# Banded attention and a dropless mixture of experts on one core: attention in steps of two units, the gate once per batch, and a fixed second expert whose weights are fetched into attention memory

## The chip, the core and the metric

The kernel runs on one core of one Trainium2 chip. A core has five engines that run their own instruction streams and meet at semaphores: TensorE (PE, matrix products; its weight loads are shown apart as PEld), VectorE (DVE), ScalarE (ACT), GpSimd (POOL) and SyncE (SP, which here only issues DMAs). Sixteen DMA engines move data between the device memory and the on-chip memory.

The metric is the device time of one execution in microseconds (us), lower is better; a kernel's time is the median of three executions. The profile comes from one further execution with the hardware profiler on.

## What is computed

The reference, cut to what matters. All numbers are float32.

```python
B, H, S, D = 4, 8, 768, 64            # batch, heads, tokens, head size
scores = q @ k.T / sqrt(D)            # per batch and head
keep = (key < n_global) | (0 <= query - key < n_local)     # 8 global keys, 96 local keys
scores += -slope[h] * dist            # dist = query-key, or n_local for a global key that is not local
a = softmax(where(keep, scores, -1e9)); attn = a @ v
x = attn.transpose(0, 2, 1, 3).reshape(3072, 512)          # one row per token

logits = x @ w_gate                   # 512 x 8
e = argmax(logits); gate = softmax(logits)[e]              # one expert of 8 for each token
y = relu(x @ w1[e]) @ w2[e]           # 512 -> 1024 -> 512, for the tokens of each expert
out = gate * y
```

Each expert gets as many tokens as chose it. With the given inputs the counts of experts 0 to 7 are 455, 416, 361, 397, 367, 410, 395 and 271. The kernel has fixed capacities `CAPS = (464, 416, 416, 400, 400, 368, 368, 272)` and a general, slower path behind a test, which these inputs do not take in either version.

## The kernel before

**Attention.** A unit is (batch b, pair of heads j, two blocks of 128 queries c); there are 4 x 4 x 3 = 48 units. `scores(n)` makes transposed scores, keys on partitions, with 64-row matmuls for the two heads; ACT takes the exponential and DVE multiplies by the bias-and-mask factors. `attend(n)` multiplies by the values (full 128-row matmuls), and DVE divides by the sums. `turn(n)` transposes the unit's output with the identity for the gate. Units are worked one at a time, each stage some units behind the one before:

```python
for n in range(nu + 1):                          # nu = 48
    if c == 1: load(pr + 3)                      # q and k of a pair of heads, pr = 4*b + j
    scores(n)
    turn(n - 4)
    logits(n - 5)                                # acts only where j == 3: three units of a batch
    attend(n - 2)
    logits_sum(n - 5)                            # likewise
    if c == 0: turn_qk(pr + 1)                   # two DVE transposes of the loaded q and k
    if c == 1: keys_at(...)                      # ACT copies
    if c == 2: turn_v(pr + 1)                    # ACT copies
    if c == 1: load_v(pr + 2)
    # one batch later, at units 6 and 8 of the batch:
    spread(b2); spread_sum(b2)
```

**Gate and places.** For each group of 256 tokens, four products of 32 columns each, side by side in the array, give partial logits, ACT copies them, and two more products with a 0/1 matrix add the four parts. `gate(b)` then runs once for a batch on DVE. `spread(b)` finds each token's place in its expert's list:

```python
def logits(n):
    for kc in range(KC):                         # KC = 4
        nc.tensor.matmul(pq[32*kc:32*kc+32, :], lhsT=wg_sb[:, kc, :], rhs=xl[:, kc, :])  # 256 columns
    nc.scalar.copy(out=lq, in_=pq)
def logits_sum(n):
    for t in range(2):
        nc.tensor.matmul(pl[:, t, :], lhsT=lq[:, P*t:P*t+P], rhs=gsum)
    nc.vector.tensor_copy(out=Ls[b][:, 2*c:2*c+2, :], in_=pl)
    if c == NB // 2 - 1: gate(...)
def spread(b):                                   # NB = 6 blocks of 128 tokens
    nc.tensor.matmul(pr, lhsT=tri, rhs=Mb, start=True, stop=False)
    for c in range(NB - 1):
        nc.tensor.matmul(pr[:, c+1:NB, :], lhsT=ones, rhs=Mb[:, c:c+1, :] ...)   # five products
    if b > 0: nc.tensor.matmul(pr, lhsT=ones, rhs=Macc ...)                      # counts of earlier batches
    # ... DVE: positions, then the tables mv and oh for spread_sum
```

**End of attention.** The tokens of expert 0 that are known after three batches are gathered early, and their work is cut into 16 pieces that fill TensorE while the routing of the last batch is worked out on DVE. POOL issues a gather of 32 rows per indirect DMA.

```python
            spread_sum(B - 1); half_0(1); order()        # order: experts 1..7 ranked by their counts
            work(1); fetch_0(1); settle(); work(1)
            rows_of(...); take(1)                        # 13 gathers for the expert that comes second
            identify(); sort_acc(1, gslot_s); fit(); work(5)
            turn_x(...); work(4)
```

**Experts.** Two sets of weight tiles take turns. `w1_second` and `w2_second` lie in a pool that is opened after attention's pools are closed, so in memory that attention used.

```python
def fetch(p, i):                       # i = 0: w1, four DMAs of 512 KB; i = 1: w2, one of 2 MB
    ids[p] = nc.values_load(ids_s[...])          # which expert, read from memory by SP
    if i == 0:
        loads = expert_w1(ws[p % 2][0], bass.ds(ids[p], 1))
        if p == 1: behind(loads[0], taken[len(taken) // 2], ...)   # after the 7th of the 13 gathers
    else: nc.sync.dma_start(ws[p % 2][1], ...)
def sort(p):                           # DVE transposes of the gathered rows of expert p
    turn_x(xes[p], xqs.pop(p), pieces_of(CAPS[ORDER[p]]))

fetch(1, 0); fetch(1, 1); ground(); sort(1)
hidden(0); plan(2); turn = result(0)             # the rest of expert 0: 208 slots
for p in range(1, E):
    hidden(p, turn)                    # 8 x 4 matmuls, ACT relu; pace() lets gathers out one by one
    fetch(p + 1, 0)
    sort(p + 1)
    plan(p + 2)
    turn = result(p)                   # 4 x 8 matmuls, DVE copies yT, then transposes and scatter
    fetch(p + 1, 1)
```

Of the kernel before, what the change touches and what calls it, by code (L numbers as in the profile page):

```python
# [29 lines left out]
def kernel(  # L30
# [27 lines left out]

    x_tok = nc.dram_tensor("x_tok", (N * NJ, P), F32)
# [22 lines left out]
    q_first = consts.tile([P, NB, 2, D], F32)  # L82
# [48 lines left out]

    tokid = consts.tile([P, NC], F32)
    iota(tokid, [[P, NC]], -N, 1)
# [5 lines left out]
    def later_constants():  # L139
# [13 lines left out]
        nc.vector.tensor_copy(out=j_of, in_=j_i)  # L153
        nc.vector.memset(wg_sb, 0.0)
        nc.sync.dma_start(wg_sb[:, :, 0:E], moe_w_gate.rearrange("(kc p) e -> p kc e", p=P))

    gsum = sel[:, 0:E]

    M_ec = consts.tile([P, E, NC], F32)
    M_ce = consts.tile([P, NC, E], F32)  # L160
    rk_all = consts.tile([P, NB, E + 1], F32)
    nc.vector.memset(rk_all[:, :, E:E + 1], 0.5)
    Macc = consts.tile([P, E], F32)
# [8 lines left out]
    NR = E - 1  # L172
# [5 lines left out]
    idx_0 = [consts.tile([P, 1, 2], I32, name=f"idx_0{i}") for i in range(2)]  # L178
    gslot_0 = [consts.tile([P, 1, 2], F32, name=f"gslot_0{i}") for i in range(2)]
    rows_0 = [consts.tile([P, 2 * TB], I32, name=f"rows_0{i}") for i in range(2)]  # L180
# [93 lines left out]
    def plan(p):  # L274
        if p < E:
            r = ORDER[p] - 1
            xqs[p] = xq_s[p % 2]
            cols = rows_s[:, NQ * TB * r:NQ * TB * r + NQ * TB]
            for i in range(pieces_of(CAPS[r + 1])):
                pending.append((xqs[p], cols, i))  # L280
# [10 lines left out]
    taken = []  # L291

    def take(p):
        plan(p)
        while pending:
            taken.append(gather_one(*pending.pop(0)))

    scatters = []

# [24 lines left out]
    def result_0(po, q, f0, nf, later=None):  # L324

        for fc in range(f0, f0 + nf):
            nc.tensor.matmul(po, lhsT=hT_0[q][:, fc, :], rhs=w2_0[:, 0, fc, :],  # L327
                             start=(fc == 0), stop=(fc == FC - 1))
        if f0 + nf == FC:
            scaled(f"y_0_{q}", P, po, gslot_0[0][:, 0, q:q + 1], idx_0[0][:, 0, q:q + 1], later)  # L330
# [18 lines left out]
    def banded_attention():  # L349
        with ExitStack() as actx:  # L350
            mp = actx.enter_context(tc.tile_pool(name="maskb", bufs=1))
            xlp = actx.enter_context(tc.tile_pool(name="xlb", bufs=3))
            xrp = actx.enter_context(tc.tile_pool(name="xrb", bufs=5))
            ldp = actx.enter_context(tc.tile_pool(name="ldb", bufs=2))
# [3 lines left out]
            xp = actx.enter_context(tc.tile_pool(name="xpb", bufs=3))  # L358
# [17 lines left out]
            def load(pr):  # L376
                b, j = divmod(pr, NJ)
                ts = []
                for nm, src in (("q", q), ("k", k)):
                    t = ldp.tile([P, S // 32, 32], F32, tag=nm, name=f"{nm}b_{pr}")  # L380
# [65 lines left out]
            far = mp.tile([P, 2, P], F32, name="farb")  # L446
# [18 lines left out]
            Ls = {}  # L465
            xls = {}
# [6 lines left out]
            def scores(n):  # L473
# [12 lines left out]
                e = ep.tile([P, 2, 512], F32, tag="e", name=f"e_{n}")  # L486
# [40 lines left out]
            def turn(n):  # L527
                b, j, c = units[n]
                xr = xrs[b, c]
                px = ps_m.tile([P, 2, P], F32, tag="m", name=f"px_{n}")  # L530
                for t in range(2):
                    nc.tensor.transpose(px[:, t, :], xr[:, t, P * j:P * j + P], ident)  # L532
                if j == 0:
                    xls[b, c] = xlp.tile([P, KC, 2 * P], F32, tag="xl", name=f"xl_{b}_{c}")
                nc.scalar.copy(out=xls[b, c][:, j, :], in_=px.rearrange("p t c -> p (t c)"))
                if j == NJ - 1:
                    store(S * b + 2 * P * c, 2, xrs.pop((b, c)))

            def logits(n):

                b, j, c = units[n]
                if j < NJ - 1:
                    return
                xl = xls.pop((b, c))
                pq = ps_m.tile([P, 2 * P], F32, tag="m", name=f"pq_{n}")
                for kc in range(KC):
                    nc.tensor.matmul(pq[32 * kc:32 * kc + 32, :], lhsT=wg_sb[:, kc, :], rhs=xl[:, kc, :],  # L547
                                     start=True, stop=True)
                lq = xp.tile([P, 2 * P], F32, tag="lq", name=f"lq_{n}", bufs=2)
                nc.scalar.copy(out=lq, in_=pq)  # L550
                st["l", n] = lq

            def logits_sum(n):
                b, j, c = units[n]
                if j < NJ - 1:
                    return
                lq = st.pop(("l", n))
                pl = ps_m.tile([P, 2, E], F32, tag="m", name=f"pl_{n}")
                for t in range(2):
                    nc.tensor.matmul(pl[:, t, :], lhsT=lq[:, P * t:P * t + P], rhs=gsum, start=True, stop=True)  # L560
                if c == 0:
                    Ls[b] = gp.tile([P, NB, E], F32, tag="L", name=f"L_{b}")
                nc.vector.tensor_copy(out=Ls[b][:, 2 * c:2 * c + 2, :], in_=pl)
                if c == NB // 2 - 1:
                    gate(b, Ls.pop(b), gp, M_ce[:, NB * b:NB * b + NB, :])

            def spread(b):

                Mb = M_ce[:, NB * b:NB * b + NB, :]
# [3 lines left out]
                for c in range(NB - 1):  # L573
                    nc.tensor.matmul(pr[:, c + 1:NB, :], lhsT=ones,
                                     rhs=Mb[:, c:c + 1, :].to_broadcast([P, NB - 1 - c, E]),
                                     start=False, stop=(b == 0 and c == NB - 2))
                if b > 0:
                    nc.tensor.matmul(pr, lhsT=ones,
                                     rhs=Macc.rearrange("p (o e) -> p o e", o=1).to_broadcast([P, NB, E]),
                                     start=False, stop=True)  # L580
                Mt = gp.tile([P, 2, NB, E], F32, tag="Mt", name=f"Mt_{b}")
                for i, f in enumerate((tokid, gates)):
# [17 lines left out]
                                        op=ALU.is_equal)  # L600
                mv = gp.tile([P, NB, 2, E, NQ], F32, tag="mv", name=f"mv_{b}", bufs=1)
# [9 lines left out]
                Mv = Mb.rearrange("p c e -> p e c")  # L611
                if b == 0:
                    nc.vector.tensor_reduce(out=Macc, in_=Mv, axis=AX.X, op=ALU.add)
                else:
                    per = gp.tile([P, E], F32, tag="per", name=f"per_{b}")
                    nc.vector.tensor_reduce(out=per, in_=Mv, axis=AX.X, op=ALU.add)
                    nc.vector.tensor_tensor(out=Macc, in0=Macc, in1=per, op=ALU.add)
# [14 lines left out]
            def half_0(i):  # L632

                f = gp.tile([P, 1, 2], F32, tag="first", name=f"first_{i}")
                nc.vector.tensor_copy(out=f, in_=acc[:, 0, 0:1, 2 * i:2 * i + 2])
                st["w", i] = wrap(gp, f"_0{i}", 2, f[:, 0, :], idx_0[i][:, 0, :])
                nc.vector.tensor_copy(out=gslot_0[i], in_=acc[:, 1, 0:1, 2 * i:2 * i + 2])

            def fetch_0(i):
                rows_of(ps_m, f"_0{i}", 2, st.pop(("w", i)), rows_0[i])  # L640
# [4 lines left out]
            def count_0():  # L645
                c2 = ps_m.tile([P, E], F32, tag="m", name="c2")
                nc.tensor.matmul(c2, lhsT=ones, rhs=Macc, start=True, stop=True)
                nc.vector.tensor_scalar(out=early, in0=c2[:, 0:1], scalar1=2.0 * P, scalar2=None, op0=ALU.is_ge)  # L648

            fill = []  # L650
            later = []
# [21 lines left out]
            def order():  # L673

                cn = ps_m.tile([P, E], F32, tag="m", name="cn")
                nc.tensor.matmul(cn, lhsT=ones, rhs=Macc, start=True, stop=True)
# [5 lines left out]
                k7 = key[:, 1:E]  # L682
# [11 lines left out]
            def identify():  # L694
# [4 lines left out]
                                        in1=iota_p[0:1, 1:E].rearrange("p (o e) -> p o e", o=1).to_broadcast([1, NR, NR]),  # L699
# [4 lines left out]
            def sort_acc(i, to):  # L704
# [5 lines left out]
                    in1=acc[:, i, 1:E, :].rearrange("p e q -> p q e").rearrange("p (o q) e -> p o q e", o=1).to_broadcast([P, NR, NQ, NR]),  # L710
# [8 lines left out]
            def fit():  # L719
# [3 lines left out]
                nc.vector.tensor_copy(out=cs[:, 0:1], in_=cnt[:, 0:1])  # L723
                sized = gp.tile([P, NR, NR], F32, tag="cmp", name="sized")
                nc.vector.tensor_tensor(out=sized, in0=R,
                                        in1=cnt[:, 1:E].rearrange("p (o e) -> p o e", o=1).to_broadcast([P, NR, NR]),
                                        op=ALU.mult)
                nc.vector.tensor_reduce(out=cs[:, 1:E], in_=sized, axis=AX.X, op=ALU.add)
# [12 lines left out]
            weights_0 = [lambda f0=f0: nc.sync.dma_start(w2_0[:, :, f0:f0 + 1, :], w2v[:, 0:1, f0:f0 + 1, :]) for f0 in range(FC)]  # L741
            weights_0 += [lambda e=e, kc=kc: nc.sync.dma_start(w1_0[32 * e:32 * e + 32, :, kc:kc + 1, :], w1v[e, :, 0:1, kc:kc + 1, :])
                          for e in range(NJ) for kc in range(KC)]
            for n in range(nu + 1):
                if n < nu:
                    b, j, c = units[n]
                    pr = b * NJ + j
                    if c == 1 and pr + 3 < B * NJ:
                        load(pr + 3)
                    scores(n)  # L750
                    if n == 2:
                        later_constants()
                    if n % 3 > 0 and 8 <= n < 44:
# [3 lines left out]
                if 0 <= n - 4 < nu:  # L757
                    turn(n - 4)
# [417 lines left out]
```

## Time and profile before

| What | Value |
|---|---|
| Time, median of three executions | 543.34 us (543.27 to 544.06) |
| Execution with the profiler on | 556.98 us, of which 555.3 us from the first to the last instruction |
| Mean granted TensorE clock in it | 0.986 |
| PE busy, PEld busy | 527.4 us, 391.7 us |
| DVE, ACT, POOL busy | 201.7 us, 132.6 us, 138.3 us |
| Data moved | 71.97 MB, mean 130 GB/s |

The profile page gives the busy time of each engine, a strip of 40 time slices, the DMA queues, the chain of work that ended last, and the costliest groups of instructions. A group names the source line, the engine, the operation and the tiles; "idle before" is the time in which the engine had nothing to do just before those instructions, with what ended most of it. The trace behind the page answers narrower questions: who waited for whom, what each engine did in a stretch of time, and the chain of waits in order of time. The busy time of a matmul is taken from its start to a modelled end, so overlapping matmuls can fill a stretch in which the array is not at its peak; the distance from one start to the next says more.

The stages of this run: attention takes from the start to about 174 us, the end of attention with the pieces of expert 0 until about 214 us, and the rest of the experts until 548 us.

### The profile page before, as it was taken

The page shows a single profiled execution, that of the slowest core. Times are in us where ns is not written, and L with a number is a line of the kernel's source. Part 1 is how long each engine was busy: PE and PEld are TensorE (multiplying, and loading weights), DVE is VectorE, ACT ScalarE, POOL GpSimd, SP SyncE. Part 2 cuts the span into 40 slices and gives each one's busy share as a digit, 9 for nine tenths or more (in the row PEclk, how much of TensorE's full clock was granted, in tenths as well). Part 3 has the DMA queues.
Part 4 walks back from the last instruction along what each step waited for, and adds up shares of the span by engine and source line. Part 5 has one row for each costly group of instructions (what it writes and reads, how often), then busy time and mean ns, then how long its engine had stood idle before and what let it go on. Part 6 is the DMA issues. An engine that isn't in the chain of part 4 may idle for free.

```text
span 555.3 us, 8124 instructions
## 1 busy us (share of the span) xinstructions
PE 527.4 (95%) x3130; PEld 391.7 (71%) x3130; DVE 201.7 (36%) x509; ACT 132.6 (24%) x263; POOL 138.3 (25%) x161
## 2 busy tenths in 40 slices
PE   4999999999999998599999999999999999999994
PEld 3988898899898965595555555555555876666694
DVE  4758687687684443112013101211301303111012
ACT  4666456555552200101101100100110100101100
POOL 5000000000007067234224423513511716402002
PEclk9999999999999999699999999999999999999998
DMA  9999999999903014995446174372543776101001
GB/s 145 146 156 178 234 176 175 231 161 159 256 6 124 31 30 93 297 187 201 98 90 223 34 159 141 114 156 70 183 107 64 234 147 216 48 0 53 3 1 60
DMA packets 145185, 71.97 MB, mean 130 GB/s; under 512 B 126656, under 2 KB 126660, under 8 KB 145136
## 3 DMA queue, kind: packets, MB, share of 16 engines
q1 hardware_dynamic: 137344, 58.16, 50.0%
q0 software_dynamic: 5264, 12.59, 7.5%
q10 hardware_dynamic: 2528, 0.59, 0.7%
q8 instruction: 27, 0.44, 0.4%
q14 instruction: 22, 0.18, 0.1%
HBM read 59.00 MB, written 12.65 MB: 129 GB/s over the span
## 4 chain that ended last, share of the span: by engine, by line
PE 85%; DMA 5%; SPq 2%; issue 2%; DVE 2%; another core or an unknown queue 2%; POOL 1%; ACT 0%; POOLq 0%; DVEq 0%; ACTq 0%
PE po L1082 26%; PE ph L1039 26%; PE o L516 12%; PE s L484 7%; PE ph L320 3%; PE px L532 3%; PE po L327 2%; PE pt L1072 2%; SPq L384 2%; DMA xq_s<-x_tok,rows_s 2%; DMA kb<-in_k_dram 1%; PE pq L547 1%; PE pi L624 1%; PE pl L560 1%
## 5 line engine op out<-in xcount | busy, mean ns | idle before, releaser
L259 POOL DMA_INDIRECT xq_s<-x_tok,rows_s x85 | 85.4, 1005 | 151.4 <-DVE yT L1084 103.6
L1041 ACT ACTIVATE hT<-ph 128x416 f32<-128x416 f32 (+4 forms) x64 | 29.6, 467 | 294.3 <-PE ph L1039 270.1
L1039 PE MATMUL ph<-xe,w_first 128*128 128x208 f32 (+3 forms) x256 | 78.7, 465 | 8.9 <-ACT hT L1041 8.9
L1082 PE MATMUL po<-hT,w_second 128*128 128x416 f32 (+4 forms) x320 | 80.7, 412 | 2.1 <-DVE yT L1084 2.1
L1039 PE MATMUL ph<-xe,w_second 128*128 128x416 f32 (+3 forms) x256 | 80.2, 469 | 0.0
L1082 PE MATMUL po<-hT,w_first 128*128 128x208 f32 (+3 forms) x256 | 75.5, 456 | 0.0
L1082 PEld LDWEIGHTS po<-hT,w_second 128*128 128x128 f32 x320 | 56.0, 190 | 26.3 <-issue 10.2
L1039 PEld LDWEIGHTS ph<-xe,w_first 128*128 128x128 f32 x256 | 49.0, 197 | 35.2 <-issue 10.0
L516 PE MATMUL o<-vt,e 128*128 128x128 f32 x384 | 72.6, 278 | 0.0
L1039 PEld LDWEIGHTS ph<-xe,w_second 128*128 128x128 f32 x256 | 48.0, 190 | 28.1 <-issue 9.9
L1082 PEld LDWEIGHTS po<-hT,w_first 128*128 128x128 f32 x256 | 47.7, 190 | 27.1 <-issue 10.2
L270 DVE STREAM_TRANSPOSE xe<-xq_s 128x128 f32<-128x128 f32 x85 | 22.8, 293 | 117.7 <-DMA xq_s<-x_tok,rows_s 112.5
L516 PE MATMUL o<-va,e 128*128 128x128 f32 x320 | 62.8, 278 | 0.0
L1084 DVE COPY yT<-po 128x416 f32<-128x416 f32 (+6 forms) x36 | 17.0, 481 | 125.6 <-PE po L1082 125.6
L259 POOL DMA_INDIRECT xq<-x_tok,rows x15 | 17.3, 1154 | 181.0 <-DVE early L648 160.5
L516 PEld LDWEIGHTS o<-vt,e 128*128 128x128 f32 x384 | 57.5, 194 | 1.5 <-issue 1.2
L487 ACT ACTIVATE e<-s 128x1024 f32<-128x1024 f32 (+1 forms) x48 | 45.5, 947 | 46.1 <-PE s L484 46.0
L516 PEld LDWEIGHTS o<-va,e 128*128 128x128 f32 x320 | 48.7, 193 | 2.6 <-issue 2.5
L301 POOL DMA_INDIRECT out_dram<-y,idx_s x25 | 24.4, 975 | 74.4 <-DVE y L309 69.9
L498 DVE TENSOR_TENSOR e<-e,Wb 128x1024 f32<-128x1024 f32 x32 | 38.8, 1211 | 10.9 <-ACT e L487 10.8
L484 PE MATMUL s<-qT,kT 64*128 64x128 f32 x384 | 40.7, 290 | 0.9 <-ACT qT L419 0.9
L484 PE MATMUL s<-qT,kA 64*128 64x128 f32 x320 | 35.7, 301 | 2.0 <-ACT kA L403 2.0
(163 smaller groups left out, 439.1 us busy)
## 6 DMA issues: line engine op xcount, KB each, us to landing
w_second<-in_moe_w_dram SPq DMA_DIRECT2D x16, 512.0 KB
w_second<-in_moe_w_dram SPq DMA_DIRECT2D x4, 2048.0 KB
x_tok<-xr SPq DMA_DIRECT2D x24, 256.0 KB
w_first<-in_moe_w_dram SPq DMA_DIRECT2D x12, 512.0 KB
w_first<-in_moe_w_dram SPq DMA_DIRECT2D x3, 2048.0 KB
vt<-in_v_dram SPq DMA_DIRECT2D x31, 192.0 KB
qb<-in_q_dram SPq DMA_DIRECT2D x60, 96.0 KB
kb<-in_k_dram SPq DMA_DIRECT2D x60, 96.0 KB
```

The source lines that it names most:

```text
L259: return nc.gpsimd.indirect_dma_start(out=xq[:, i, :], out_offset=None, in_=x_tok[0:NJ * top, :], in_offset=bass.IndirectOffsetOnAxis(ap=c ...
L270: nc.vector.transpose(xe[:, :, 32 * i:32 * i + 32], xq[:, i, :].rearrange("p (k q) -> p k q", k=KC))
L301: p = nc.gpsimd.indirect_dma_start(out=out[:, :], out_offset=bass.IndirectOffsetOnAxis(ap=where, axis=0), in_=y[0:rows, :], in_offset=None ...
L320: nc.tensor.matmul(ph[:, P * f:P * f + P], lhsT=w1_0[:, 0, kc, c0:c0 + P], rhs=xe_0[:, kc, P * q:P * q + P], start=(kc == 0), stop=(kc == ...
L484: nc.tensor.matmul(ps[:, h, P * m:P * m + P], lhsT=lhsT, rhs=qT[r, P * i:P * i + P], start=True, stop=True)
L487: nc.scalar.activation(e[:, :, 0:w], ps[:, :, 0:w], AF.Exp, scale=D ** -0.5)
L498: nc.vector.tensor_tensor(out=eh, in0=eh, in1=W[:, 2 * j:2 * j + 2, P:3 * P].rearrange("p h (o c) -> p h o c", o=1).to_broadcast([P, 2, 2, ...
L516: nc.tensor.matmul(po[:, t, h, :], lhsT=pt[:, h, P * m:P * m + P], rhs=(vt if own else va)[:, c0:c0 + P], start=(m == mine[0][0]), stop=(m ...
L1039: nc.tensor.matmul(ph[:, 0:C], lhsT=w1t[:, 0, kc, P * fc:P * fc + P], rhs=xe[:, kc, 0:C], start=(kc == 0), stop=(kc == KC - 1))
L1041: done = nc.scalar.activation(hT[:, fc, 0:C], ph[:, 0:C], AF.Relu)
L1082: nc.tensor.matmul(po[:, 0:c1 - c0], lhsT=w2t[:, 0, fc, P * dc:P * dc + P], rhs=hT[:, fc, c0:c1], start=(fc == 0), stop=(fc == FC - 1))
L1084: pace(2 if dc == 0 else 1, nc.vector.tensor_copy(out=yT[:, dc, c0:c1], in_=po[:, 0:c1 - c0]))
```

## The change

It has four parts.

1. **Steps of two units.** The loop takes two units at a time: both units' scores, then both units' transposes of an earlier step into one PSUM tile and one ACT copy, then both units' products with the values.
2. **The gate once per batch.** The transposed outputs of a whole batch are kept; 16 products of 192 columns, four side by side, sum over the 512 inputs in PSUM, and a DVE transpose brings the logits to the tokens' partitions. The partial-logit copies and the summing products go. The order of the tokens on partitions changes with it (`tokid`).
3. **Places by a scan.** A DVE scan along the blocks of a batch gives the running counts `C_b`, so `spread` needs two products and not seven, and `Macc` goes. The tables `mv` and `oh` become a function of their own, `tables`, which is issued one step later.
4. **Expert 1 is always second.** It has the fixed capacity 416; experts 2 to 7 are ranked as before. Its weights lie in tiles of their own, and during attention these tiles serve as attention's buffers (q and k loads, the kept outputs, one of the four exponentials). They are loaded at the end of attention, before the places of the last batch are known. Its row list comes with that of expert 0. In the expert stage the weights are then fetched one expert further ahead, and the DVE transposes of the next expert's rows are moved from before `result(p)` into it.

The diff, cut to its core:

```diff
+    w1_1 = consts.tile([P, 1, KC, F], F32, name="w1_second")
+    w2_1 = consts.tile([P, 1, FC, DM], F32, name="w2_second")
...
-            for n in range(nu + 1):
+            for n0 in range(0, nu, 2):
+                two = (n0, n0 + 1)
+                if n0 > 0 and c < 2 and pr + 1 < B * NJ:
+                    turn_qk(pr + 1)
+                for n in two:
+                    if c == 1 and pr + 3 < B * NJ: load(pr + 3)
+                    scores(n)
+                if n0 >= 4:
+                    turn(n0 - 4)                 # now for two units
+                    for n in two: attend(n - 2)
+                if b > 0 and m == 2: logits(b - 1)
+                if b > 0 and m == 4: spread(b - 1)
+                if 0 < b and m == (4 if b == B - 1 else 6): tables(b - 1)
+                if 0 < b and m == (6 if b == B - 1 else 8): spread_sum(b - 1)
...
+            def logits(b):
                 for kc in range(KC):
-                    nc.tensor.matmul(pq[32 * kc:32 * kc + 32, :], lhsT=wg_sb[:, kc, :], rhs=xl[:, kc, :], ...)
-                nc.scalar.copy(out=lq, in_=pq)
+                    for g in range(TB):          # TB = 4, QS = 192
+                        nc.tensor.matmul(pq[32 * g:32 * g + 32, :], lhsT=wg_sb[:, kc, :],
+                                         rhs=xl[:, kc, QS * g:QS * g + QS], start=(kc == 0), stop=(kc == KC - 1))
+                nc.vector.transpose(L, pq)
+                gate(b, ...)
+                nc.vector.tensor_tensor_scan(out=C_b[b] ..., data0=first0 ..., data1=M_b[b] ...)
-            def logits_sum(n): ...
...
             def spread(b):
                 nc.tensor.matmul(pr, lhsT=tri, rhs=Mb, start=True, stop=False)
-                for c in range(NB - 1): nc.tensor.matmul(pr[:, c + 1:NB, :], lhsT=ones, ...)
-                if b > 0: nc.tensor.matmul(pr, lhsT=ones, rhs=Macc ...)
+                nc.tensor.matmul(pr, lhsT=ones, rhs=C_b[b][:, :, 0:NB] ..., start=False, stop=True)
...
+            turn(nu - 2)
+            expert_w1(w1_1, slice(1, 2))
+            work(1)
+            logits(B - 1)
+            nc.sync.dma_start(w2_1, w2v[:, 1:2, :, :])
+            work(1); spread(B - 1); tables(B - 1); work(2); spread_sum(B - 1); half_0(1); work(1)
+            fetch_0(1)                           # row lists of expert 0's rest and of expert 1
+            order(); work(2); settle(); work(1); rows_of(...)
...
-            fetch(1, 0); fetch(1, 1); ground(); sort(1)
-            hidden(0); plan(2); turn = result(0)
+            ground(); sort(1, 0, 1)
+            hidden(0); fetch(2, 0); plan(2); turn = result(0); fetch(2, 1)
             for p in range(1, E):
                 hidden(p, turn)
-                fetch(p + 1, 0)
-                sort(p + 1)
+                fetch(p + 2, 0)
                 plan(p + 2)
                 turn = result(p)                 # with sort(p + 1, ...) after its 2nd and 3rd yT copies
-                fetch(p + 1, 1)
+                fetch(p + 2, 1)
```

## The prediction, made before the result was known

> **What bounds the kernel now.** I read the page's first part, then PE's waits, then the chain of waits in order of time, then two stretches up close. PE's share of busy time, from the page:
>
> ```profile
> PE 527.4 (95%) x3130; PEld 391.7 (71%) x3130; DVE 201.7 (36%) x509; ACT 132.6 (24%) x263; POOL 138.3 (25%) x161
> ```
>
> A PE at 95% need not be at its peak, so I also asked who PE waited for. Columns: waiter, what ended the wait, total us, times, longest.
>
> ```profile
> PE ph L1039 <- ACT hT L1041: 8.9, 1, 8.9
> PE first L417 <- POOL grp L145: 4.8, 1, 4.8
> PE po L1082 <- DVE yT L1084: 2.1, 1, 2.1
> PE s L484 <- ACT kA L403: 2.0, 1, 2.0
> ```
>
> Apart from the start there are two waits after attention: one of 8.9 us and one of 2.1 us. Within attention PE hardly waits (28.57 us busy of 29.80 in the stretch 12 to 41.8, then 42.20 of 42.20 for a batch), so there **the order and number of PE's own instructions are the time**. The chain in the stretch 96 to 111 us (start, length, what):
>
> ```profile
> 95.89 0.37 PE px L532 x2
> 96.26 0.57 PE pq L547 x8
> 96.83 1.53 PE o L516 x12
> 98.36 0.35 PE pl L560 x4
> 98.71 0.87 PE s L484 x12
> 99.58 0.37 PE px L532 x2
> ...
> 108.30 0.37 PE px L532 x2
> 108.67 1.34 PE o L516 x12
> 110.01 0.87 PE s L484 x12
> 110.88 0.26 PE px L532
> ```
>
> Both parts are the same short unit (12 `o`, 12 `s`), the first with logits, the second without. From px to px the first takes 99.58 - 95.89 = 3.69 us, the second 110.88 - 108.30 = 2.58 us. Logits cost PE 1.11 us in each of three units of a batch.
>
> The 8.9 us need care. The chain in the stretch 200 to 240:
>
> ```profile
> 217.96 0.34 ACT hT L1041
> 218.31 10.21 another core or an unknown queue
> 228.54 0.35 ACT hT L1041
> 228.93 7.79 PE ph L1039 x32
> ```
>
> ACT's second relu of expert 0's rest starts 10.2 us after the first, although its matmuls were issued by 217. Meanwhile SP issues expert 1's w1, with 9.8 us for four DMAs that take 1.85 us for later experts. The chain calls the releaser unknown. It is tempting to say "expert 1's weights are late, and the change removes it", but nothing on this chain reads them.
>
> More: the profiled execution spans 555.3 us, the timed ones take 543.3. PE runs the experts evenly (8 matmul records of 416 columns in 2.79 us), so an execution 12 us shorter can hardly have come from faster matmuls. The gap, with the slow clock after it, does: 8.9 us idle, and PE at 0.50 to 232.8, which costs (232.8 - 228.9)/2 = 1.9 us, together 10.8. My reading, at 4 to 1: **this gap belongs to the profiled execution and isn't in the 543.3**.
>
> **What the Trainium skill says.** "Perfetto Trace Analysis", Identifying the Most-Contended Engine, warns that PE's busy share misleads and names weight-load busy time; here that is 71% against 95%, so I use distances between starts. "TensorEngine Tiling (Array Packing)", Key Properties, says that a change of tiling mode drains the array. The trace agrees: in the PE timeline groups start every 0.22 to 0.23 us, but 0.32 apart on the last `o` to the first `s` (109.62, 109.94), on the first `s` (to 110.26), and on the last `s` to px (110.49, 110.81): 0.29 us a unit for going into 64-row products and out. "TensorE: Matmul & The Clock Gate", What's actually happening, says that an idle array falls to half clock; after the 8.9 us the clock record does show 0.50. "DMA: Bandwidth & Descriptors", Issuing engines are not separate DMA queues, says that all queues interleave on the same 16 engines; see the gather below.
>
> **Part by part.**
>
> *Two units a step.* Of 48 switches into 64-row products and back, 24 remain. I count 22 saved (two are at the start, where loads and a slow clock rule): 22 x 0.29 = 6.4 us. Work between `scores` and `attend` only grows, so PE gets no shorter leash to ACT and DVE.
>
> *Gate once a batch.* Before: 3 x 1.11 = 3.33 us. After: 16 products, 8 rounds (two passes each of four inputs) of four side by side. A pq group of two rounds of 256 columns takes 0.57, some 0.14 of it for switching, so 0.215 a round and 0.16 for 192 columns: 8 x 0.16 + 0.15 = 1.45 us. Saved 1.9 a batch, 5.6 for three.
>
> *Places.* `spread` stands between `o` (111.24 + 1.79 = 113.03) and the next `s` (114.53): 1.50 us for 14 records, 0.107 each; the first has 12. With 4 records it is 0.43. Saved 0.85 + 1.07 + 1.07 = 3.0 us. The tables and `spread_sum` (1.29 us) stay.
>
> Sum in attention: 6.4 + 5.6 + 3.0 = 15.0. *What may eat it:* DVE. It is busy 31 to 32 us of a batch's 42; when a batch shrinks to about 37.5 us it is at 83%, and its order is fixed. After the logits it does the gate (some 2.4 us from the durations of the tail: 0.2 each), then a turn of q and k (1.9), two products with W (2.4), and only then the divisions. Reckoned with these durations, the divisions of two steps end 0.2 to 0.8 us before px needs them. I take off 1.5 us for that, and 1 for the first batch, where loads of v hold ACT (3.6 us at 30.7). Left: 12.5.
>
> *End of attention.* The same 16 pieces fill PE; logits and spread save 1.9 + 1.1, but one piece (1.9 us) now stands against the DVE chain from logits to counts (some 2.6 us): a new wait of 0.8. Net 2.1.
>
> *Expert 1's weights.* In an undisturbed run before, PE would do expert 0's rest from 214.4: 64 records of hidden work at 0.176 us = 11.3, then 11.25 for the result, so expert 1 would start at 236.9. Its w1, issued from 217.2, is 2 MB at the 207 GB/s of that stretch: 10 us, there by 228. **It was hidden already**; loading it at 177 buys nothing by itself. A fixed second expert changes no work: expert 1 has 416 tokens, the largest count of the seven, and was second anyway.
>
> *Sort within the result.* The 2.1 us are this. DVE, which works in order, waited for the last gather of the seventh expert's rows before the yT copies that free PSUM:
>
> ```profile
> 458.48 0.31 DVE L270 STREAM_TRANSPOSE xe<-xq_s 128x128 f32<-128x128 f32 x1 [10.84 <-DMA xq_s<-x_tok,rows_s]
> 458.71 1.10 DVE L1084 COPY yT<-po 128x272 f32<-128x272 f32 x3
> ```
>
> The gather was issued at 448.1 and landed 10.3 us later, beside a 2 MB w1 load issued at 447.5. Other experts have it too (9.1 to 9.9 us of waiting), but their results take 20 us and PE does not notice; the sixth has 272 slots and 3.8 us a product. With the transposes behind the second and third copy the wait is off PE's path: 2.1 us saved. The weights' earlier fetch adds no bytes, and PE never waited for them.
>
> Sum: 12.5 + 2.1 + 2.1 = 16.7; 543.3 - 16.7 = **526.6 us**.
>
> **Rivals.** (1) *The gap is in the timed runs too.* For: the profile shows it, and the change removes the w1 load from that spot. Against: the 12 us between profile and timing. Then about 11 us more go, to 516. (2) *DVE or ACT becomes the bound in attention.* For: 83% and a fixed order. Against: the work between dependent steps is longer than before. If each of three batches loses 3 us, 534. (3) *Loads become the bound.* DMA share is about 1.0 to 150 us. But a pair's q and k arrive in 6 to 7.5 us once started and pairs start some 9 us apart, with a turn 7 to 12 us after the last packet; this is slack. If wrong, attention stays as long as it is: 539. (4) *The early loads delay gathers at attention's end* as w1 delayed the gather above: 4 MB near 180 to 200 us, beside gathers of tokens with 15 us to spare. Nothing or 2 to 3 us.
>
> **Range and chances.** Between rivals 2 and 3 on the one side and rival 1 at one in five on the other, 515 to 533 should hold it 8 times in 10. The 2% line is 532.5: faster by more than that 0.85, within 0.14, slower 0.01.
>
> **What would show it.** A batch of attention at 37 to 38.5 us, not 42.3; attention's last `o` ending near 163 to 166 us, not 177.7; `s` records in runs of 28 or 32; PE waits in attention below 3 us in all; no wait of PE for yT near expert six; expert 0's rest to expert 1 without a gap, and a profiled span within 3 us of the timed median if the gap was the profiler's. I am wrong if PE waits for xr, e or qT repeatedly, if the loads fall behind the turns, or if the profile after has the odd gap elsewhere and the timings don't follow it.

## The result, and the profile after

The changed kernel takes **527.98 us** (median of 4 runs, 527.35 to 529.82), the kernel before 543.7 on the same chip (543.27 to 544.06). The ratio is 0.9717, 95% interval 0.9691 to 0.9743: 15.7 us less, where 16.7 were predicted.

From the profile page of the changed kernel: busy time, share of the span and instructions of each engine:

```profile
PE 506.7 (96%) x3076; PEld 380.6 (72%) x3076; DVE 197.2 (38%) x506; ACT 126.5 (24%) x227; POOL 136.7 (26%) x161
```

TensorE lost 20.7 us of busy time, its share hardly moved, and it has only 54 records fewer. The waits of TensorE in the changed kernel (waiter, what ended the wait, total us, times, longest):

```profile
PE first L428 <- POOL sel_i L152: 4.7, 1, 4.7
PE s L493 <- ACT kA L414: 2.0, 1, 2.0
PE px L545 <- DVE early L645: 1.6, 1, 1.6
PE pw L268 <- DVE gslot L633: 1.3, 1, 1.3
PE s L493 <- ACT qT L430: 0.9, 1, 0.9
```

The two waits that stood after attention before, 8.9 us for hT and 2.1 for yT, are not here. Two new ones, 1.6 and 1.3 us, stand in attention's last batch. Both are for VectorE, which in the trace works without a break from 131.3 to 149.8 us there: the tables of the third batch come one step earlier than those of the other batches, and the first list of expert 0's tokens follows close behind.

The chain of waits of the changed kernel in the stretch 54 to 64 us, and the next batch's logits from the same view (start, length, what):

```profile
54.98 1.44 PE pq L559 x32
56.42 1.99 PE s L493 x32
58.40 0.59 PE px L545 x4
58.99 3.13 PE o L528 x28
62.12 0.18 PE pr L575 x2
62.29 0.22 PE pr L576 x2
...
92.40 1.44 PE pq L559 x32
```

The same piece of work in the kernel before, two units of it, has these lines (each unit also has a `px` of 0.37 us, as in the prediction's lines):

```profile
115.99 1.79 PE o L516 x16
117.78 1.09 PE s L484 x16
...
119.23 1.34 PE o L516 x12
```

Side by side they show what the change does to TensorE's order: `s` and `o` in runs of up to 32 where they had at most 16, the logits once per batch in 1.44 us, and the places in 0.18 + 0.22 = 0.40 us. Two runs of `s` of 1.09 us have become one of 1.99, two `px` of 0.37 one of 0.59, and `o` takes 1.79 + 1.34 = 3.13 us as it did: **0.34 us less for each step of two units**. From pq to pq a batch takes 92.40 - 54.98 = 37.4 us, before 42.3 in the mean of two. The same view at the start of the experts:

```profile
185.62 12.05 PE po L340 x28
197.67 11.25 PE ph L1046 x64
208.92 11.25 PE po L1089 x64
...
220.29 1.85 PE ph L1046 x5
```

Expert 0's rest is 64 records of hidden work in 11.25 us and 64 of the result in 11.25, with nothing in between. The profiled span is 525.5 us, within 3 of the median.

### The profile page after: what moved, and what is told of

Read it like the earlier page. It is cut to its first block, busy times and chain, and to the rows that moved or that the text cites. A ratio compares the mean times of both kernels' runs of the same rounds, so it can differ in the third digit from the quotient of the medians.

```text
span 525.5 us, 7951 instructions
## 1 busy us (share of the span) xinstructions
PE 506.7 (96%) x3076; PEld 380.6 (72%) x3076; DVE 197.2 (38%) x506; ACT 126.5 (24%) x227; POOL 136.7 (26%) x161
## 4 chain that ended last, share of the span: by engine, by line
PE 94%; DVE 2%; POOL 1%; DMA 1%; issue 0%; SPq 0%; ACT 0%; POOLq 0%
PE po L1089 29%; PE ph L1046 29%; PE o L528 14%; PE s L493 8%; PE px L545 3%; PE po L340 3%; PE ph L333 2%; PE pt L1079 2%; PE pq L559 1%; DMA x_tok<-xr 1%; PE pi L618 1%; PE first L428 1%; DVE e L506 0%; DVE kT L429 0%; DVE w_second L510 0%
## 5 line engine op out<-in xcount | busy, mean ns | idle before, releaser
L273 POOL DMA_INDIRECT xq_s<-x_tok,rows_s x72 | 72.6, 1009 | 133.4 <-DVE yT L1091 58.9
L1046 PE MATMUL ph<-xe,w_first 128*128 128x208 f32 (+3 forms) x256 | 76.5, 456 | 0.0
L1089 PEld LDWEIGHTS po<-hT,w_second 128*128 128x128 f32 x320 | 56.1, 190 | 23.9 <-issue 10.2
L1089 PEld LDWEIGHTS po<-hT,w_first 128*128 128x128 f32 x256 | 47.7, 190 | 27.1 <-issue 10.2
L528 PE MATMUL o<-vt,e 128*128 128x128 f32 x288 | 53.9, 278 | 0.0
L528 PE MATMUL o<-va,e 128*128 128x128 f32 x240 | 46.9, 277 | 0.0
L528 PEld LDWEIGHTS o<-vt,e 128*128 128x128 f32 x288 | 43.2, 195 | 0.2 <-issue 0.2
L314 POOL DMA_INDIRECT out_dram<-y,idx_s x21 | 20.5, 976 | 71.8 <-DVE y L322 68.8
L499 ACT ACTIVATE e<-s 128x1024 f32<-128x1024 f32 (+1 forms) x36 | 33.0, 943 | 18.2 <-PE s L493 18.2
L528 PEld LDWEIGHTS o<-va,e 128*128 128x128 f32 x240 | 36.9, 194 | 0.1
L493 PEld LDWEIGHTS s<-qT,kT 64*128 64x128 f32 x384 | 30.2, 196 | 2.2 <-ACT qT L430 1.3
L510 DVE TENSOR_TENSOR e<-e,Wb 128x1024 f32<-128x1024 f32 x24 | 28.8, 1213 | 7.4 <-ACT e L499 7.3
```

Source lines behind the costliest of these rows:

```text
L273: return nc.gpsimd.indirect_dma_start(out=xq[:, i, :], out_offset=None, in_=x_tok[0:NJ * top, :], in_offset=bass.IndirectOffsetOnAxis(ap=c ...
L314: p = nc.gpsimd.indirect_dma_start(out=out[:, :], out_offset=bass.IndirectOffsetOnAxis(ap=where, axis=0), in_=y[0:rows, :], in_offset=None ...
L493: nc.tensor.matmul(ps[:, h, P * m:P * m + P], lhsT=lhsT, rhs=qT[r, P * i:P * i + P], start=True, stop=True)
L499: nc.scalar.activation(e[:, :, 0:w], ps[:, :, 0:w], AF.Exp, scale=D ** -0.5)
L510: nc.vector.tensor_tensor(out=eh, in0=eh, in1=W[:, 2 * j:2 * j + 2, P:3 * P].rearrange("p h (o c) -> p h o c", o=1).to_broadcast([P, 2, 2, ...
L528: nc.tensor.matmul(po[:, t, h, :], lhsT=pt[:, h, P * m:P * m + P], rhs=(vt if own else va)[:, c0:c0 + P], start=(m == mine[0][0]), stop=(m ...
```

## The experiments

The three chips of the experiments took longer for both kernels than the runs of the result did (556 to 558 us for the kernel before, 545 to 547 for the changed one), so each experiment is measured against the changed kernel, or the kernel before, run in the same conditions, and not against 527.98. Intervals below are of the ratio to the kernel before, measured beside each kernel.

Theory: the time is TensorE's own order, above all the switches between products of 64 rows and of 128, the logits and the places. The rivals: the early weights or the gap ahead of the experts carry a large part, or the transposes within the result do.

**The changed kernel again** (no edit), as the measure for the next three.

> The changed kernel itself, as the mark for the others on this chip. Both theories: 527 to 529 us, 0.971 of the kernel before.

Measured 547.01 us, 0.9806 (0.9769 to 0.9842); the kernel before beside it took 557.93. A batch is the same 37.4 us as in the result's run, and from the start of expert 1 to TensorE's last product it is 297.4 us against 297.2. The span is 21.0 us longer (546.5 against 525.5), and 13.4 of these lie between hidden(0) and hidden(1), the first products of expert 0's rest and of expert 1: 36.1 us against 22.7. Most of that is one wait. TensorE's waits in this run:

```profile
PE ph L1046 <- ACT hT L1048: 10.2, 1, 10.2
...
PE o L528 <- DVE recips L532: 2.2, 1, 2.2
```

So the wait for hT, which the prediction had put down to the profiled execution, is in the changed kernel too, with expert 1's weights long loaded.

**One unit at a time within a step:**

```diff
                     scores(n)
+                    if n0 >= 4 and n == n0:
+                        attend(n0 - 2)
 ...
-                    for n in two:
-                        attend(n - 2)
+                    attend(n0 - 1)
```

> The changed kernel, with the products with the values of one unit put between the two units' scores, so that TensorE goes into 64-row products and out again twice a step instead of once. Same instructions, another order. Theory A (each way in and out costs 0.29 us of draining): 22 steps x 0.29 = 6.4 us more than the changed kernel, 534 us. Theory B (the order is free, the gain is all in fewer gate and place products): within 1 us of the changed kernel. Theory C (longer steps help by hiding waits on ScalarE and VectorE): more time again, but then as waits of TensorE in the profile and not in the distances between starts.

Measured 550.66 us, 0.9875 (0.9845 to 0.9905), 3.7 above the changed kernel. The chain of waits of this kernel, stretch 58 to 70 and the next batch:

```profile
60.24 1.44 PE pq L559 x32
61.68 1.09 PE s L493 x16
62.77 1.98 PE o L528 x16
...
66.43 1.34 PE o L528 x12
...
100.16 1.44 PE pq L559 x32
```

The instructions are the same, in runs of 16 and 12; a run of `o` that follows `s` directly takes 1.98 us and not 1.79. The batch takes 100.16 - 60.24 = 39.9 us against 37.4: 2.5 us for six switches in and out more, **0.42 us each**, where the prediction had 0.29. The chain here is TensorE alone, so it isn't a wait for another engine. This is not quite the old order: there `px` stood between `s` and `o`, and here the transposes of two units stay together; so 0.42 is the price of this order, and what the change saved is the 0.34 read above. The timed difference, 3.7 us, is neither Theory A's 6.4 nor Theory B's 1. It is smaller than 22 x 0.42 = 9.2 because the last batch gives some back: at the first product of the third batch's tables (154.2 us against 146.4) this kernel is 7.8 us behind, at that of the fourth's (187.6 against 184.0) 3.6. There TensorE waits for VectorE in the changed kernel, 1.3 us for gslot and 2.2 for recips, and in this slower one it doesn't.

**The places by seven products**, with the gate still once per batch:

```diff
-                nc.tensor.matmul(pr, lhsT=ones, rhs=C_b[b][:, :, 0:NB]..., start=False, stop=True)
+                for c in range(NB - 1):
+                    nc.tensor.matmul(pr[:, c + 1:NB, :], lhsT=ones, rhs=Mb[:, c:c + 1, :].to_broadcast(...), ...)
+                nc.tensor.matmul(pr, lhsT=ones, rhs=M_b[b][:, :, 0:1]....to_broadcast([P, NB, E]), ...)
```

> The changed kernel with the old seven products in the place sums (the triangle, five with ones, one for the earlier batches' counts) in place of two. Five more products of two records each, 0.107 us a record, four batches: 4 x 1.07 = 4.3 us more if TensorE's instruction count is the time (532 us). If the path there is VectorE's (the rival): less than 1 us more.

Measured 550.6 us, 0.9883 (0.9853 to 0.9914), 3.6 above the changed kernel. The chain of waits of this kernel:

```profile
65.80 0.18 PE pr L575 x2
65.98 1.06 PE pr L577 x10
67.04 0.28 PE pr L579 x2
```

These are 1.52 us in place of 0.40, and the batch is 97.10 - 58.66 = 38.4 us by the starts of pq, 1.0 longer. That is the predicted 1.07 a batch. With the fourth batch's at the end of attention that makes some 4 us, beside the 3.6 timed.

**Expert 1's weights late**, behind the middle one of expert 1's gathers, as before the change:

```diff
-            expert_w1(w1_1, slice(1, 2))          # after turn(nu - 2)
-            nc.sync.dma_start(w2_1, ...)          # after logits(B - 1)
 ...
+            loads = expert_w1(w1_1, slice(1, 2))  # ahead of ground()
+            behind(loads[0], taken[len(taken) // 2], ...)
+            nc.sync.dma_start(w2_1, w2v[:, 1:2, :, :])
```

> The changed kernel with expert 1's weights loaded where the kernel before loaded them: w1 behind the seventh gather of its rows, w2 after that. Theory A (they were hidden anyway): within 1 us of the changed kernel, since w1 would be there some 9 us ahead of use. Rival (the 8.9 us gap of the first profile is what the early load removes): 9 to 11 us more, 537 to 539 us.

Measured 548.72 us, 0.9854 (0.9825 to 0.9883). That is 1.7 above the changed kernel with overlapping intervals, and its profiled execution is shorter (544.7 us against 546.5). TensorE's waits have the 10.2 us for hT as before and none for weights; from hidden(0) to hidden(1) it takes 35.6 us, against 36.1 with the weights early. The weights neither cause the gap nor end it. Whether late weights would be in time without a gap can only be estimated: in this run the load of both starts at 206.6 us and the DMA engines fall idle between 225 and 227, while hidden(1) would start at 203.9 + 22.6 = 226.5 with the distance of the result's run. w1, which is issued first, would then be there, and w2 is needed only with the result, over 20 us later.

**The transposes ahead of the result**, not within it:

```diff
-                        if p > 0 and 0 < dc < KC - 1:
-                            sort(p + 1, dc - 1, KC - 2)
 ...
                 fetch(p + 2, 0)
+                sort(p + 1, 0, 1)
```

> The changed kernel with the next expert's row transposes put back ahead of the result products, all else as it is. Theory A: the wait of 2.1 us on the copies out of PSUM at the sixth expert comes back and nothing else: 2 us more. Rival (moving the transposes gained nothing, or the earlier weight fetch changed when the last gather lands): under 0.5 us.

Measured 546.64 us, 0.9828 (0.9806 to 0.985), against 547.01 and 0.9806 (0.9769 to 0.9842). The intervals overlap, and the kernel before beside the two differs by 2.1 us itself (555.87 and 557.93), so the timing alone can't decide about 2 us. The trace does: expert 1 to the last product takes 297.3 us against 297.4, and TensorE's waits name no yT. Moving the transposes gained nothing.

**The kernel before again.**

> The kernel before, profiled a second time. Theory A (the 10 us gap after the first relu of expert 0's rest belongs to that one profiled execution): a profiled span of 541 to 545 us without the gap, and the 2.1 us wait for the yT copies still there. Rival (the gap is in every execution): the gap again, at the same place.

Measured 556.09 us, 1.0005 (0.9989 to 1.0022), with a profiled span of 554.4. All of TensorE's waits in this run after attention's start:

```profile
PE ph L1039 <- ACT hT L1041: 8.7, 1, 8.7
...
PE pl L560 <- DVE L L563: 0.7, 1, 0.7
PE px L532 <- DVE xr L523: 0.6, 1, 0.6
PE ph L320 <- DVE xe L270: 0.3, 1, 0.3
```

The gap is there again, as the rival had it, at least on this chip. **There is no wait for yT.** From expert 1 to the last product this run of the kernel before takes 297.4 us, as long as the changed kernel; the profile shown in the prediction had 299.6. So the 2.1 us are not in every execution of that kernel.

**The first list of tokens one unit later**, to break up the unbroken work of VectorE in the last batch:

```diff
-                if n0 == nu - 4:
-                    fetch_0(0)
-                    count_0()
                 if n0 >= 4:
                     turn(n0 - 4)
                     for n in two:
                         attend(n - 2)
+                        if n == nu - 4:
+                            fetch_0(0)
+                            count_0()
```

> The changed kernel with the row list of expert 0's first tokens worked out after the first unit's products with the values in that step, instead of before the transposes. In the changed kernel's trace TensorE waits there 1.29 us for the list and 1.61 us for VectorE's release of a PSUM tile. Theory A (VectorE's fixed order makes the wait, and it is on the path): 2 to 2.9 us less, 525 us. Rival (the gathers start later and the pieces of expert 0 wait instead): no gain, or 1 to 2 us more.

Measured **538.93 us**, 0.9695 (0.9672 to 0.9718), 7.7 below the 546.64 of the kernel beside it, the one with the transposes ahead, whose end of attention is the changed kernel's. TensorE's waits in this kernel:

```profile
PE ph L1046 <- ACT hT L1048: 10.2, 1, 10.2
...
PE px L545 <- DVE xr L535: 0.7, 1, 0.7
```

The waits for gslot (1.3), for the rows (1.6) and for recips (2.2) are gone, 0.7 is new, and attention's last `o` starts at 162.6 us instead of 171.9. That is more than the 5.1 - 0.7 = 4.4 us of waits; without them TensorE also stays at full clock here, where the changed kernel has stretches at a mean of 0.76. The windows of 5 us around them (TensorE's busy time follows the length, the granted clock is the number before the DMA share), first the changed kernel of the first experiment:

```profile
150.00:155.00 5.00, 2.53 (x17) 2.47 (x18) 2.96 (x10) 1.91 (x4) 1.41 (x2) 0.90 0.00 1
155.00:160.00 5.00, 5.00 (x49) 4.88 (x49) 1.21 (x4) 0.91 (x2) 3.79 (x4) 0.76 0.20 52
```

and the same stretch with the list later:

```profile
150.00:155.00 5.00, 5.00 (x61) 4.86 (x59) 3.33 (x9) 2.22 (x4) 1.72 (x2) 1.00 0.02 6
155.00:160.00 5.00, 5.00 (x48) 4.89 (x45) 3.49 (x6) 1.85 (x3) 4.08 (x4) 1.00 0.20 52
```

What remained was the wait for hT. In the timeline of the changed kernel's first run among the experiments, TensorE, then ScalarE, then GpSimd (start, length, engine, line, operation; in brackets the idle time before and what ended it):

```profile
205.09 4.38 PE L1046 MATMUL ph<-xe,w_first 128*128 128x208 f32 x24
219.69 6.53 PE L1046 MATMUL ph<-xe,w_first 128*128 128x208 f32 x19 [10.22 <-ACT hT L1048]
219.29 0.81 ACT L1048 ACTIVATE hT<-ph 128x208 f32<-128x208 f32 x3 [27.40 <-remote]
215.58 1.01 POOL L314 DMA_INDIRECT out_dram<-y,idx  x1 [0.30 <-issue]
```

TensorE does three groups of hidden work and stops, as all three buffers are full. The first is done at 206.7 us, but ScalarE begins its relu only at 219.3. The trace also keeps when semaphores changed: TensorE's update for that group is recorded at 219.22, 12.6 us after its last product. GpSimd had then just ended an unbroken row of 22 indirect DMAs, from 188.0 to 216.6 (13 gathers of expert 1's tokens among them), each some 1.0 us and 0.3 apart. In the result's run the same row of 22 stands from 180.4 to 208.8, and the first relu there starts 0.1 us after the first group's last product. This gave a second theory: on these chips the row of indirect DMAs holds up the updates. Three kernels test it.

**Expert 1's gathers paced**, two behind each relu of expert 0's rest:

```diff
-        take(1)
+        plan(1)
 ...
-                    pace(1 if fc < FC - 1 else len(pending), done)
+                    pace((2 if p == 0 else 1) if fc < FC - 1 else len(pending), done)
 ...
-                        if p > 0 and 0 < dc < KC - 1:
+                        if 0 < dc < KC - 1:
 ...
             ground()
-            sort(1, 0, 1)
             hidden(0)
```

> The changed kernel, with the 13 gathers of expert 1's tokens handed out two behind each relu of expert 0's rest instead of back to back ahead of it, and the transposes of those tokens put behind the second and third copy of expert 0's result. GpSimd's burst of 22 indirect DMAs at the end of attention shrinks to 9. Theory (a long burst of indirect DMAs on GpSimd holds up the semaphore updates of the other engines; the wait of 8.7 to 10.2 us for hT at the start of the experts is that): the wait is gone or under 2 us, the distance from hidden(0) to hidden(1) falls from 36.0 to 23 to 25 us, and the time is some 10 to 12 us below that of the changed kernel in this same call. Rival (the wait comes from something else at that place, such as expert weights being loaded or the store of attention's rows): the wait stays near 10 us and the time within 2 us of the changed kernel's. If the chip shows no such wait in the changed kernel beside it, nothing is told apart, and I expect the two within 2 us.

> The changed kernel itself, beside the others of this call. On a chip like that of the earlier experiments 547 us with a wait for hT of about 10 us; on one like that of the result 528 us without it. It is the measure for the two kernels with paced gathers.

Measured: paced 541.06 us, 0.9701 (0.9662 to 0.9739); the changed kernel beside it 545.19, 0.9768 (0.973 to 0.9806). Pacing brings 4.1 us, not the 10 to 12 expected. TensorE's waits in the paced kernel:

```profile
PE po L1089 <- issue: 2.9, 3, 1.1
...
PE ph L1046 <- DVE xe L284: 1.0, 1, 1.0
```

and in the changed kernel beside it:

```profile
PE ph L1046 <- issue: 3.5, 4, 1.7
PE ph L1046 <- DVE xe L284: 2.9, 1, 2.9
...
PE ph L1046 <- ACT hT L1048: 1.6, 1, 1.6
```

The hold-up looks different even from run to run of one kernel (here 8.0 us in several pieces, before 10.2 in one). With pacing it moved into the result of expert 0's rest, to where the gathers went, and shrank. Neither reading won: hidden(0) to hidden(1) takes 29.0 us against 31.5, and 22.7 in the result's run.

**Both together**, paced gathers and the later list:

> The changed kernel with both: the first list of expert 0's tokens started one unit later, which brought 8 us on the slower chip (538.9 against 547.0 and 546.6), and expert 1's gathers paced. If the long burst is the cause of the wait for hT: 8 us from the list and 10 to 12 from the pacing add up, some 527 to 529 us on a chip where the changed kernel takes 547. If it isn't: 539. On a chip where the changed kernel takes 528: 524 to 527, from the 2.9 us of waits at the end of attention alone.

Measured **532.07 us**, 0.9547 (0.9504 to 0.959): 13.1 us below the changed kernel beside it, and the version that beats both kernels here. The sum expected was 527 to 529; what is missing is pacing's part, as above.

**Without expert 1's gathers.** This leaves part of the computation out: expert 1 works on zeros, with all instructions of the other engines kept.

```diff
-        take(1)
+        plan(1)
+        del pending[:]
```

> The changed kernel without the 13 gathers of expert 1's tokens: expert 1 works on the zeros with which its buffer is filled, so its rows of the output are left out; all instructions of the other engines stay, and so do the loads and the scatters. GpSimd has 9 indirect DMAs at the end of attention and none while expert 0's rest runs. Theory (the indirect DMAs issued by GpSimd hold up the semaphore updates of the other engines on this chip): no wait of PE at the start of the experts above 0.5 us, and hidden(0) to hidden(1) in 22.5 to 23.5 us, as in the result's run, against 31 to 36 in the changed kernel and 29 with paced gathers; time 8 to 13 us below the changed kernel's in this call. Rival (the hold-up is of the place, the chip's or the loads', and only moved when the gathers moved): 29 us or more, with waits of PE for hT or for its own sequencer that add up to 5 us or more.

> The changed kernel beside it: 545 to 547 us, with 31 to 36 us from hidden(0) to hidden(1), if the chip is like that of the earlier experiments; 528 us and 22.7 if it is like that of the result, where leaving out the gathers should then change less than 2 us.

The chain of waits without these gathers:

```profile
205.09 11.25 PE ph L1047 x64
216.34 11.25 PE po L1090 x64
...
227.71 2.90 PE ph L1047 x8
...
524.90 0.76 DVE y L322
```

and of the changed kernel beside it:

```profile
206.96 3.58 PE ph L1046 x19
...
218.76 10.04 PE ph L1046 x40
228.80 11.25 PE po L1089 x64
...
240.17 1.85 PE ph L1046 x5
...
537.66 0.76 DVE y L322
```

**The gap is gone**: 227.71 - 205.09 = 22.6 us from hidden(0) to hidden(1), as in the result's run, against 240.17 - 206.96 = 33.2 beside it; TensorE is busy in all of the 50 us from 190 to 240. Its work ends 12.8 us earlier (524.90 against 537.66). The timed gain is only 2.5 us (544.52 against 547.05; 0.975 and 0.9777), below the 8 to 13 of the theory: after its last DMA GpSimd's closing instructions take longer, one drain alone 9.6 us instead of 1.6. Why leaving out 13 gathers does that stays open.

## Why the prediction was right, step by step

*TensorE's order bounds attention: right.* A batch takes 37.4 us (37 to 38.5 predicted) and attention's last `o` starts at 164.4 and ends at 164.6 (163 to 166). Attention lost 177.4 - 164.4 = 13.0 us; 12.5 were predicted, from two errors that nearly cancel.

- *Two units a step* was a little too small: 0.34 us a step by the lines of the two kernels, not 0.29. For 22 steps that is 7.5 us and not 6.4.
- *The gate*: 1.44 us for predicted 1.45; *the places*: 0.40 for 0.43, and seven products cost 1.0 us a batch in the experiment for the predicted 1.07. Both right. In a batch in which all parts are at work (before from the logits at 96.26 us to those at 138.66) 6 x 0.34 + 1.9 + 1.1 = 5.0 us stand against 42.4 - 37.4 = 5.0 measured.
- *What eats it*: 7.5 + 5.6 + 3.0 = 16.1 us stand against 13.0, so 3.1 were eaten where 2.5 were taken off. The first batch, for which 1 of these was set aside, has no new wait. TensorE's two waits for VectorE in the last batch are 2.9 us; behind them its granted clock is 0.73 from 150 to 155 us, some 1.3 us more, so these parts fit to about 1 us. The place was wrong: not the divisions of every batch, but the tables and the list of the last. The experiment with the list one unit later shows it. On its chip attention's last `o` starts at 178.4 in the kernel before, 171.9 in the changed one and 162.6 with the later list. So there the change gained 6.5 us in attention, and with the crowded stretch of VectorE broken up 15.8, next to the 16.1 of the parts.

*End of attention*: from the last `o` to hidden(0) it was 177.4 to 214.2, 36.8 us, and is 164.4 to 197.5, 33.1: 3.7 us less where 2.1 were predicted. The 3.0 us of logits and places are there. The new wait of 0.8 isn't: the places follow the piece of work before them within some 0.3 us, while the kernel before had two waits of 0.3 there in the profile (0.7 and 0.3 in its second run), which the prediction had not counted.

*Expert 1's weights: right.* They neither make nor end a wait of TensorE in any of these runs, early or late.

*The sort within the result: wrong.* The step "the wait is off PE's path: 2.1 us saved" took a wait seen in one execution for a property of the kernel. It is not in the second run of the kernel before, nor with the transposes ahead of the result again. It was worth 0 in these runs.

*The gap of 8.9 us: half right.* By the sums it isn't in the 543.3 us, as the prediction held against rival 1: the parts without it come to 16.7 us, and 15.7 were measured, so none of these is left for it. But "belongs to the profiled execution" was wrong: on the experiments' chips it came in the profile of each kernel that has these gathers at that place, and the timed runs there were longer as well. That 543.3 and 555.3 differed showed that one execution was unlike the others; it didn't show that the profiler was why. Its 557.0 us is what the kernel before takes in the timed runs of the experiments' chips (553.6 to 560.5), so it may have run in their conditions; the record doesn't tell.

The sum: 13.0 + 3.7 + 0 = 16.7 us between the two profiles, leaving out the gap; that this is the very sum predicted is luck, as its parts were 12.5, 2.1 and 2.1. Between the medians it is 15.7. The 1.0 left over is not explained; the profile before was of an execution with the gap. Of the rivals, VectorE as the bound came true in the last batch alone (2.9 us), slow loads and delayed gathers did not.

## What to carry to other kernels

Where an engine is busy all the time, ask what its order costs: grouping the same products into longer runs gave 0.34 us a step here. Reading it off single gaps in a timeline gave 0.29, and undoing it 0.42: an undoing is a sure measure only where it brings back the old order, so compare the whole runs of products of the two orders as well. A wait seen in one profile is a guess about the kernel until a second execution has it too, and one that the timed runs don't contain must not be booked as a gain. When a change shortens one engine's part, look for the place where another engine's fixed order is densest; moving one list by one unit there gave 7.7 us on a chip where the whole change had given 11 (557.93 to 547.01).

## What the runs showed of the hardware

On the chips of the experiments, updates of semaphores by TensorE were recorded up to 12.6 us after the product that made them, while GpSimd issued a long row of indirect DMAs; ScalarE and then TensorE stood still, and TensorE went on at a clock of 0.5 in places (0.50 to 0.57 in windows after the gap). Without the 13 gathers of that row the hold-up is gone (22.6 us instead of 33.2), with the gathers spread it is smaller and elsewhere. So these gathers are needed for it there. They are not enough: in the result's run the same row of 22 delayed nothing. What differs between the chips or their conditions, and whether the gathers' issue, their transfers or the transposes that wait for them do it, stays open.
